# Keeping attention's output in float32, two load queues at the start, and the last output in halves

## Chip, core and metric

The kernel runs on one core of a Trainium2 chip (trn2). The time is the device time of one execution in microseconds (us). TensorE is called PE, VectorE DVE, ScalarE ACT, GpSimd POOL and SyncE SP; on SP only DMA issues appear.

## The reference

Causal attention with B = 2, H = 12, S = 448, D = 64, then two mixture blocks without routing. All arrays are float32.

```python
scores = scale * np.matmul(q, k.transpose(0, 1, 3, 2))
scores = np.where(mask, -1000000000.0, scores)
attn = np.exp(scores - np.max(scores, axis=-1, keepdims=True))
attn = attn / (np.sum(attn, axis=-1, keepdims=True) + 1e-09)
x = np.matmul(attn, v)            # reshaped to 896 tokens x 768
h = x @ w_in                      # 768 -> 2048
x = (h - np.tanh(h)) @ w_out      # 2048 -> 768
a = x @ w_a                       # 768 -> 1536
b = x @ w_b
out = a * b @ w_out2              # 1536 -> 768
```

## The kernel before

**Layout.** Two heads are stacked on 128 partitions, so attention works on 12 pairs (b, p). The output of pair (b, p) is a tile of 128x448 of x: six row blocks kk of 128 features and two batches B0, B1 of 448 tokens. Every float32 product is made of three matmuls over a high and a low part (`matmuls`, L323): high by high, weight-high by x-low, weight-low by x-high. So every operand needs a high part (a cast, on ACT) and a low part (a subtraction, on DVE or POOL). From the second group of the first block on, products run as a 2x2 scheme with seven products, which needs sums and differences of blocks of x.

**Weights.** A part of a weight goes through a pipeline: `load_part` (L175, two SP DMAs into one of three raw buffers), `magnitude` (L188, an ACT cast into `top`), `bits` (L197, a DVE operation that puts the float32 value into a tile `t` and frees the raw buffer), `split_high` (L292, ACT, `wh`) and `split_low` (L301, `wl`, POOL in attention, DVE later). `wh` and `wl` are a ring of five; PE frees an entry when its last matmul with it is done.

**Attention.** Its order is written out by hand in the table ORDER (L23–48), a string of steps. `S` are scores, `L` is mask and minimum on DVE (L431), `X` the exponential on ACT (L440), `T` a transpose on PE (L454) and `C` the copy of its result (ACT L462, DVE L464), `V` the values (L480), `D` the division (L522, L524), which writes x to a tile `x` and its high part to `xh`; `J` makes the low part `xl` (L534). `q`, `k`, `v` are loads on SP (L376, L382). Steps without a pair number are spare steps: `w` two loads of weights, `m` magnitude, `b` bits, `h` and `l` the splits, `f` two matmuls of the first block's hidden layer for batch B0, `g` what follows it. Ahead of the table stand the first loads and WARM = 6 matmuls of zeros (L561, L562).

**After attention** the scheduler orders what is not bound. For kk = 0, 1, 2, `x_sums` (L680) puts x together again as xh + xl for row blocks kk and kk + 3, two adds of 128x896 (L685), and makes four differences of 128x448 from them (L653). `x_terms` (L694) splits these into high and low parts with `halve` (L649, L650). The first group of four hidden blocks runs as plain products for B1, and then, for each of the six blocks dm of w_out, two products of 12 matmuls (four hidden blocks by three), each in a PSUM bank named `s`, `t`, `o` or `h`; ACT copies its bank away (`ypart`, L834) before the bank is used again. Tiles of `g` (`gwh`, `gwl`, 128x896) come from a pool with six of each.

**The end.** The last loop adds up the seven products per row block; for m = 4 `kept` (L883, ACT copy) and `put` (L888, SP DMA) send 128x448 of the output. The very last one is m = 4, n = 2.

Of the kernel before, what the change touches and what calls it, by code (L numbers as in the profile page):

```python
# [9 lines left out]
F32 = mybir.dt.float32  # L10
# [30 lines left out]
L0.9 T20.8 T30.8 S3.10 L2.9 C30.8 X0.9 C20.8 S01.10 b g h V0.8 Q2.11 L3.10 J.6 X1.9 Q3.11 g L1.10 V1.8 v.10 D.8  # L41
T31.9 X2.9 A.9 w H.11 T30.9 C31.9 C30.9 f I.9 l f X3.10 w f T01.9 L0.10 W.9 f f Q1.11 m C01.9 w T21.9 g C21.9
T20.9 C20.9 f f T00.9 m g f f R.9 J.7 X1.10 S2.10 X0.10 S3.11 K.9 C00.9 L2.10 g g L3.11 V1.9 V0.9 X2.10 g S01.11
S2.11 T20.10 f f L0.11 C20.10 g A.10 J.8 L1.11 T31.10 T21.10 X1.11 b C31.10 f I.10 f X0.11 m T30.10 C21.10
T00.10 b C30.10 X3.11 f f W.10 f f D.9 C00.10 L2.11 T01.10 f w X2.11 g A.11 R.10 C01.10 I.11 g m T31.11 K.10
V1.10 W.11 V0.10 T00.11 D.10 f w C31.11 C00.11 f v.11 f T21.11 f T20.11 g f C21.11 g f f T30.11 C20.11 T01.11
C30.11 f J.9 f R.11 C01.11 b V0.11 V1.11 K.11 D.11 g J.11 H.9 g w J.10 g g H.4
# [4 lines left out]
def attention_moe_moe2(ctx, tc, q, k, v, w_in, w_out, w_a, w_b, w_o, out):  # L52
    nc = tc.nc
    B, H, S, D = v.shape
# [5 lines left out]
    WARM = 6  # L60
# [4 lines left out]
    QC = 112  # L65
    NQ = S // QC
    KD = DM // 128
    NPAIR = H // 2
# [20 lines left out]
    s3p = ctx.enter_context(tc.tile_pool(name="s3", bufs=2))  # L89
# [252 lines left out]
    def attention():  # L342
        with ExitStack() as st:
# [147 lines left out]
            def widen(i):  # L491
                r = sums.pop(i)
                sums[i] = sp.tile([QC, NQ, 2, D], F32, tag="wide", name="wide", bufs=2)
                nc.gpsimd.tensor_copy(out=sums[i], in_=r.unsqueeze(3).to_broadcast([QC, NQ, 2, D]))

# [85 lines left out]
    gh, gl, gw, g_full, made = {}, {}, {}, [], set()  # L581
    PIECES = [slice(a, min(a + 512, NT)) for a in range(0, NT, 512)]
    BATCHES = [slice(b * S, (b + 1) * S) for b in range(B)]
    B0, B1 = BATCHES

    def new_g(f):

        if not g_full:
            gh[f, 0], gl[f, 0] = [g_a.tile([128, S], F32R, tag=x, name=x) for x in ("gh", "gl")]
            return  # L590
        g = [g_full[0].tile([128, NT], F32R, tag=x, name=x) for x in ("gwh", "gwl")]
        gw[f] = g
        for b in range(B):
            gh[f, b], gl[f, b] = [t[:, BATCHES[b]] for t in g]

    def hidden(w, cs, hi, lo, h, act, dve):
# [4 lines left out]
        th = ep.tile([128, 512], F32, tag="e", name="e")[:, :n]  # L601
        gg = ep.tile([128, 512], F32, tag="e", name="e")[:, :n]
# [7 lines left out]

    held, fills, rests = [], [], []
# [16 lines left out]
    def load_parts():  # L628
# [5 lines left out]
        "h": split_high, "l": split_low,  # L634
# [7 lines left out]
    g_full.append(ctx.enter_context(tc.tile_pool(name="g2", bufs=max(GROUPS1))))  # L642
# [12 lines left out]
    def etile():  # L655
        return ep.tile([128, 512], F32, tag="e", name="e")[:, :S]
# [23 lines left out]
    def x_sums(kk):  # L680

        sums = []
        for k, tag in ((kk, "gwh"), (kk + NK, "gwl")):
            t = g_full[0].tile([128, NT], F32, tag=tag, name="xsum")
            nc.vector.tensor_tensor(out=t, in0=xh[k].bitcast(F32), in1=xl[k].bitcast(F32), op=ALU.add)  # L685
            sums.append(t)
        (b11, b12), (b21, b22) = [[t[:, cs] for cs in BATCHES] for t in sums]
        minus(b11, b12, b11)
        minus(b12, b22, b12)
        minus(b22, b22, b11)  # L690
        minus(b21, b21, b22)
        return {5: b11, 7: b12, 6: b22, 4: b21}

    def x_terms():  # L694

        for kk in range(NK):
            halve(xh[kk][:, B1], xl[kk][:, B1], sums[kk][5])
            yield
# [59 lines left out]
    def times(u, q, x, on_chip):  # L758
# [10 lines left out]
        if p not in g32:  # L769
            g32[p] = g_full[0].tile([128, NT], F32, tag=("gwh", "gwl")[b], name="g32")  # L770
# [28 lines left out]
    for gi, g in enumerate(GROUPS1):  # L799
        final = gi == len(GROUPS1) - 1  # L800
        if gi == 0:
            sums = {}
            for f in range(g):
                if f < NK:
                    sums[f] = x_sums(f)
                if f % 2 == 0:
                    two = [g_full[0].tile([128, NT], F32R, tag=x, name=x) for x in ("gwh", "gwl")]
# [92 lines left out]
    for m in LAST:  # L900
        for n, u in enumerate(quads):
# [15 lines left out]
            elif m == 7:  # L917
                add(z[n], o)
                put(2 * n + 1, B1, z[n])
            elif m == 4:  # L920
                put(2 * n + 1, B0, kept(o))
# [30 lines left out]
```

## Time and profile before

| what | value |
|---|---|
| median of 3 runs | 547.32 us (546.91 to 547.54) |
| the profiled execution itself | 546.67 us |
| span in its profile | 544.9 us |
| PE busy | 539.3 us, 99% |
| DVE, ACT, POOL busy | 437.9 (80%), 334.3 (61%), 65.4 us (12%) |
| moved by DMA | 64.94 MB, mean 119 GB/s |

The span goes from the first to the last recorded instruction; the time of the execution has a little beside it. Busy time is that of an engine's own instructions; a matmul's end is modelled, so start-to-start distances say more about PE's pace than durations. "Idle before" an instruction is the time in which its engine did nothing, with what ended it.

### The profile page before, as it was taken

To read this page: it belongs to the slowest core of one execution; us is meant where nothing else is said; L and a number is where in the kernel's file an instruction comes from. 1 tells how busy PE (TensorE), PEld (TensorE's weight loads), DVE (VectorE), ACT (ScalarE), POOL (GpSimd) and SP (SyncE) were. 2 spreads that over 40 slices of the span, in tenths; PEclk is the share of its full clock that TensorE was granted. 3 is DMA by queue.
4 is the path that set the end of the run, shared out by engine and by line. 5 is a ranking of instruction groups with operands and counts; after the bars stand their busy time and mean duration, and the time that the engine had idled before them with its cause. 6 is when DMAs were issued, how large, how long until landed. Compare 5 with 4: busy or idle time off the path is not lost.

```text
span 544.9 us, 8643 instructions
## 1 busy us (share of the span) xinstructions
PE 539.3 (99%) x3094; PEld 480.9 (88%) x3094; DVE 437.9 (80%) x855; ACT 334.3 (61%) x688; POOL 65.4 (12%) x88
## 2 busy tenths in 40 slices
PE   8999999999999999999999999999999999999997
PEld 5777788898999899899898899999999999999996
DVE  6888886499889778549879999879798879999840
ACT  6999996466768743238746464756565657356511
POOL 5689761200000000000000000000000000000000
PEclk9999999999999999999999999999999999999999
DMA  8835242145144641313741033637474531001011
GB/s 259 261 102 161 68 133 80 32 161 171 58 130 155 215 137 59 115 59 96 225 143 59 0 116 117 209 111 241 136 251 135 190 116 58 2 0 52 17 69 67
DMA packets 70827, 64.94 MB, mean 119 GB/s; under 512 B 13952, under 2 KB 70784, under 8 KB 70784
## 3 DMA queue, kind: packets, MB, share of 16 engines
q1 hardware_dynamic: 70784, 64.40, 37.3%
q8 instruction: 24, 0.39, 0.3%
q14 instruction: 19, 0.16, 0.1%
HBM read 61.63 MB, written 2.75 MB: 118 GB/s over the span
## 4 chain that ended last, share of the span: by engine, by line
PE 98%; ACT 1%; DVE 0%; issue 0%; DVEq 0%
PE s L328 43%; PE t L328 19%; PE h L328 14%; PE o L328 8%; PE o L480 5%; PE s L419 4%; PE t L454 4%; PE t L499 1%; PE h L454 1%; PE h L562 1%; ACT p L440 0%; DVE p L431 0%; ACT ypart L834 0%; ACT e L885 0%; DVE warm L355 0%
## 5 line engine op out<-in xcount | busy, mean ns | idle before, releaser
L292 ACT CAST wh<-t 128x384 fp32r<-128x384 f32 (+2 forms) x141 | 77.1, 577 | 49.3 <-PE s L328 24.4
L194 ACT CAST top<-raw 128x768 f16<-128x768 bf16 (+1 forms) x70 | 73.9, 1056 | 48.5 <-DMA raw<-in_moe_w_b 12.9
L301 DVE TENSOR_TENSOR wl<-t,wh 128x384 fp32r<-128x384 f32 (+2 forms) x136 | 82.1, 625 | 15.5 <-ACT wh L292 15.2
L214 DVE SCALAR_TENSOR_TENSOR t<-raw,top 128x768 int32<-128x768 int32 (+1 forms) x62 | 58.6, 960 | 0.4 <-ACT top L194 0.2
L440 ACT ACTIVATE p<-p,m 112x448 f32<-112x448 f32 (+3 forms) x96 | 50.0, 528 | 4.5 <-DVE m L431 4.2
L328 PE MATMUL s<-last,wh 128*128 128x448 f32 x168 | 48.4, 365 | 0.0
L328 PE MATMUL s<-xl,wh 128*128 128x448 f32 x120 | 44.0, 366 | 0.0
L328 PE MATMUL s<-xh,wl 128*128 128x448 f32 x120 | 43.5, 365 | 0.0
L328 PE MATMUL s<-xh,wh 128*128 128x448 f32 x120 | 43.4, 366 | 0.0
L431 DVE CUSTOM_DVE_ANT_0 p<-s,mask 112x448 f32<-112x448 f32 (+3 forms) x96 | 37.9, 440 | 6.3 <-PE s L419 5.7
L328 PE MATMUL s<-gwh,wl 128*128 128x384 f32 (+2 forms) x96 | 34.9, 365 | 0.0
L328 PE MATMUL s<-gwl,wh 128*128 128x384 f32 (+2 forms) x96 | 34.8, 364 | 0.0
L328 PE MATMUL s<-gwh,wh 128*128 128x512 f32 (+2 forms) x96 | 34.3, 364 | 0.0
L328 PEld LDWEIGHTS s<-last,wh 128*128 128x128 f32 x168 | 31.5, 188 | 2.6
L328 PE MATMUL s<-last,wl 128*128 128x448 f32 x84 | 30.7, 365 | 0.0
L745 DVE TENSOR_TENSOR e<-s,e 128x448 f32<-128x448 f32 x31 | 19.2, 619 | 12.7 <-PE s L328 12.4
L454 PE MATMUL t<-ident,p 112*112 112x112 f32 x195 | 27.6, 265 | 0.2 <-ACT p L440 0.2
L480 PE MATMUL o<-pt,v 112*64 112x224 f32 (+1 forms) x288 | 26.1, 326 | 0.0
L462 ACT COPY pt<-t 112x448 f32<-112x448 f32 (+1 forms) x39 | 18.5, 485 | 11.8 <-PE t L454 10.2
L649 ACT CAST last<-g 128x896 fp32r<-128x896 f32 x21 | 19.0, 942 | 10.4 <-PE t L328 4.5
L401 POOL TENSOR_TENSOR qkl<-qk,qkh 128x448 fp32r<-128x448 f32 x22 | 25.2, 1147 | 1.0
L454 PEld LDWEIGHTS t<-ident,p 112*112 112x112 f32 x195 | 19.9, 133 | 5.7 <-issue 1.1
(219 smaller groups left out, 1459.8 us busy)
## 6 DMA issues: line engine op xcount, KB each, us to landing
raw<-in_moe_w_out SPq DMA_DIRECT2D x48, 383.2 KB, 4.1
raw<-in_moe_w_in SPq DMA_DIRECT2D x32, 383.2 KB, 4.0
raw<-in_moe_w_a SPq DMA_DIRECT2D x24, 383.2 KB, 4.1
raw<-in_moe_w_b SPq DMA_DIRECT2D x24, 383.2 KB, 4.9
raw<-in_moe_w_out SPq DMA_DIRECT2D x12, 255.5 KB, 3.2
qk<-in_q SPq DMA_DIRECT2D x12, 224.0 KB, 3.8
qk<-in_k SPq DMA_DIRECT2D x12, 224.0 KB, 4.5
v<-in_v SPq DMA_DIRECT2D x24, 112.0 KB, 3.3
```

The source lines that it names most:

```text
L194: nc.scalar.copy(out=tops[i % len(tops)][:, 0:nk, :, 1], in_=top[:, :, :, 2])
L214: nc.vector.scalar_tensor_tensor(out=ts[i], in0=low[:, :, :, 0], scalar=13, in1=top, op0=ALU.logical_shift_right, op1=ALU.bitwise_or)
L292: nc.scalar.copy(out=halves[j][0], in_=x)
L301: engine.tensor_tensor(out=lo, in0=source(j), in1=hi.bitcast(F32), op=ALU.subtract)
L328: nc.tensor.matmul(o, a, b_, start=j == 0 and not go_on, stop=j == n - 1, skip_group_check=True)
L401: nc.gpsimd.tensor_tensor(out=lo[:, x], in0=qk[i][:, x], in1=hi[:, x].bitcast(F32), op=ALU.subtract)
L419: nc.tensor.matmul(sc[i, c][e], a[r, 0, cs], b_[r, 1, :n], start=x == 0, stop=x == len(terms) - 1)
L431: nc.vector.tensor_tensor_reduce(out=p[:, e], in0=s, in1=mask[:QC, S - n:], scale=-scale, scalar=3.0e38, op0=ALU.add, op1=ALU.min, accum_o ...
L440: nc.scalar.activation(out=p[:, e], in_=p[:, e], func=ACTF.Exp, bias=least[i][:, c, e:e + 1], scale=-1.0, accum_out=sums[i][:, c, e:e + 1],)
L454: nc.tensor.transpose(out=pst[:QC, x * QC:(x + 1) * QC], in_=blk, identity=ident[:QC, :QC])
L480: nc.tensor.matmul(o[64 * e:64 * e + 64, cs], vt[:, k_, e, :], p.rearrange("s c q -> s (c q)"), start=k_ == 0, stop=k_ == 2 * h + 1, skip_ ...
L745: nc.vector.tensor_tensor(out=x, in0=o, in1=x, op=ALU.add)
```

## The change

1. **x in float32.** `divide` writes x into tiles of the g ring, in float32, and they stay there. `x_sums` with its adds is gone. Its twelve differences are made in place by a generator `early_sums`, a step of which stands in ORDER as `P` (six times); the rest follow through `x_terms`.
2. **Room and order.** The g ring is split: a pool with three of each is there from the start, one with three more opens after attention, together with the `s3` pool. Tiles `e` are 448 instead of 512 wide, `wide` has one buffer instead of two, `x` is gone. In ORDER, `w`, `m` and `b` stand earlier in the last seven lines, and there is one more of each.
3. **Loads.** The host lays v out with rows of 512 numbers for a pair; from the third pair on its v is one DMA, before that two. The k of pairs 0 and 1 is issued by ACT. WARM is 5.
4. **The end.** The last output is copied and sent in two halves of 224 columns, the first by SP, the second by ACT's queue.

```diff
 ORDER = """
...
-S2.11 T20.10 f f L0.11 C20.10 g A.10 J.8 L1.11 T31.10 T21.10 X1.11 b C31.10 f I.10 f X0.11 m T30.10 C21.10
...
+g S01.11 S2.11 T20.10 m f f L0.11 C20.10 g A.10 J.8 L1.11 P T31.10 T21.10 X1.11 b C31.10 w m P f I.10 f X0.11
...
-    WARM = 6
+    WARM = 5
...
             def fetch(i, nm):
                 b, p = pairs[i]
                 if nm == "v":
-                    for e in range(2):
-                        nc.sync.dma_start(
-                            out=vs[i % NV][:, :, e, :], in_=v[b, 2 * p + e].rearrange("(c s) d -> s c d", s=QC)
-                        )
+                    for x in (slice(0, 1), slice(1, 2)) if i < 2 else (slice(0, 2),):
+                        nc.sync.dma_start(out=vs[i % NV][:, :, x], in_=v[b, p][:, :, x])
                     return
                 if nm == "q":
                     qk[i] = inp.tile([128, 2, S], F32, tag="qk", name="qk")
-                nc.sync.dma_start(
+                queue = nc.scalar if i < 2 and nm == "k" else nc.sync
+                queue.dma_start(
...
             def divide(i):
-                xs[i] = sp.tile([128, S], F32, tag="x", name="x", bufs=2)
+                b, k = pairs[i]
+                if k not in x32:
+                    x32[k] = g_tile("gwh" if k < EARLY else "gwl", F32)
+                xs[i] = x32[k][:, BATCHES[b]]
...
+    EARLY = KD // 2
+    g_early = ctx.enter_context(tc.tile_pool(name="g1", bufs=EARLY))
...
+    def g_tile(tag, dt=F32R):
+
+        n = g_count.get(tag, 0)
+        g_count[tag] = n + 1
+        pool = g_early if n % max(GROUPS1) < EARLY else g_full[0]
+        return pool.tile([128, NT], dt, tag=tag, name=tag)
...
+    def early_sums():
+
+        def minus_x(kk, x):
+            (b11, b12), (b21, b22) = [[x32[k][:, cs] for cs in BATCHES] for k in (kk, kk + EARLY)]
+            o, p, q = ((b11, b12, b11), (b12, b22, b12), (b22, b22, b11), (b21, b21, b22))[x]
+            nc.vector.tensor_tensor(out=o, in0=p, in1=q, op=ALU.subtract)
+            sums[kk] = {5: b11, 7: b12, 6: b22, 4: b21}
+
+        for kk in range(EARLY):
+            minus_x(kk, 0)
+            yield
+        for kk in range(EARLY):
+            for x in (1, 2, 3):
+                minus_x(kk, x)
+                yield
...
-    g_full.append(ctx.enter_context(tc.tile_pool(name="g2", bufs=max(GROUPS1))))
+    s3p = ctx.enter_context(tc.tile_pool(name="s3", bufs=2))
+    g_full.append(ctx.enter_context(tc.tile_pool(name="g2", bufs=max(GROUPS1) - EARLY)))
...
-    def x_sums(kk):
-
-        sums = []
-        for k, tag in ((kk, "gwh"), (kk + NK, "gwl")):
-            t = g_full[0].tile([128, NT], F32, tag=tag, name="xsum")
-            nc.vector.tensor_tensor(out=t, in0=xh[k].bitcast(F32), in1=xl[k].bitcast(F32), op=ALU.add)
...
             elif m == 4:
-                put(2 * n + 1, B0, kept(o))
+                rows = slice((2 * n + 1) * 128, (2 * n + 2) * 128)
+                for queue, cs in ((nc.sync, slice(0, S // 2)), (nc.scalar, slice(S // 2, S))):
+                    e = etile()[:, 0:S // 2]
+                    nc.scalar.copy(out=e, in_=o[:, cs])
+                    queue.dma_start(out=out[rows, cs], in_=e)
```

Three places of the order of instructions, before and after. In the rows a name is a tile, its number the instance.

SP at the very start, before:

```order
L382 DMA qk<-in_q 128x448
L382 DMA qk<-in_k 128x448
L382 DMA qk<-in_q 128x448
L382 DMA qk<-in_k 128x448
L376 DMA v_99<-in_v 112x4x64 x2
L382 DMA qk<-in_q 128x448
L382 DMA qk<-in_k 128x448
```

and after:

```order
L378 DMA qk<-in_q 128x448 x2
L373 DMA v_99<-in_v 112x4x64 x2
L378 DMA qk<-in_q 128x448
L378 DMA qk<-in_k 128x448
L373 DMA v_100<-in_v 112x4x64 x2
L182 DMA raw<-in_moe_w_in 128x3x511 x2
```

The loads of k for pairs 0 and 1 have left SP's queue; the q of pair 1 stands second, and v follows at once. ACT's queue after the change begins with them, ahead of the load of its table:

```order
L378 DMA qk<-in_k 128x448 x2
L436 ACT_TABLE_LOAD
L436 ACTIVATE p,sum<-p,m 112x448 [waits DVE_49] x2
L436 ACTIVATE p,sum<-p,m 112x336 [waits DVE_49] x2
L458 COPY pt_103<-t 112x4x112 [waits PE_49]
```

DVE just after attention, before. `wl` are the low parts of weight blocks of w_out, each the work of one split:

```order
L301 TENSOR_TENSOR wl<-t,wh 128x512
L650 TENSOR_TENSOR tl<-xsum,th 128x448
L653 TENSOR_TENSOR xsum<-xsum 128x448
L301 TENSOR_TENSOR wl<-t,wh 128x512
L214 SCALAR_TENSOR_TENSOR t<-raw,top_84 128x512
L301 TENSOR_TENSOR wl<-t,wh 128x512
L650 TENSOR_TENSOR tl<-xsum,th 128x448
L650 TENSOR_TENSOR xl<-xsum,xh 128x448
L214 SCALAR_TENSOR_TENSOR t<-raw,top_83 128x768
L650 TENSOR_TENSOR gl<-xsum,gh 128x448
L214 SCALAR_TENSOR_TENSOR t<-raw,top_84 128x768
L301 TENSOR_TENSOR wl<-t,wh 128x512
```

and after:

```order
L624 TENSOR_TENSOR gwl<-gwl 128x448 x2
L298 TENSOR_TENSOR wl<-t,wh 128x512 x3
L676 TENSOR_TENSOR gl<-gwl,gh 128x448
L211 SCALAR_TENSOR_TENSOR t<-raw,top_81 128x512
L676 TENSOR_TENSOR xl<-gwh,xh 128x448
L211 SCALAR_TENSOR_TENSOR t<-raw,top_80 128x768
L676 TENSOR_TENSOR xl<-gwh,xh 128x448 x2
L298 TENSOR_TENSOR wl<-t,wh 128x512
L612 TENSOR_TENSOR e<-h,e 128x448
L211 SCALAR_TENSOR_TENSOR t<-raw,top_81 128x768
```

The adds of 128x896 are gone, the first three `wl` stand in a row instead of being spread over other steps, and the fourth comes behind the `xl`.

PE at the third dm block, before. `gh` and `gl` are the hidden layer's parts, `o` and `t` banks:

```order
L328 MATMUL t_2005<-gl_1687,wh_1824 128x448
L328 MATMUL t_2005<-gh_1686,wl_1825 128x448
L328 MATMUL o_2134<-gh_1146,wh_1947 128x448 [waits Activation_49]
L328 MATMUL o_2134<-gl_1147,wh_1947 128x448
L328 MATMUL t_2092<-gh_1146,wh_1912 128x448 [waits Activation_49]
L328 MATMUL t_2092<-gl_1147,wh_1912 128x448
L328 MATMUL t_2092<-gh_1146,wl_1913 128x448 [waits DVE_49]
L328 MATMUL t_2092<-gh_1419,wh_1912 128x448
L328 MATMUL t_2092<-gl_1420,wh_1912 128x448
```

and after:

```order
L325 MATMUL t_1980<-gl_1680,wh_1814 128x448
L325 MATMUL t_1980<-gh_1679,wl_1815 128x448
L325 MATMUL o_2108<-gh_1137,wh_1921 128x448 [waits Activation_49]
L325 MATMUL o_2108<-gl_1138,wh_1921 128x448
L325 MATMUL o_2108<-gh_1137,wl_1922 128x448 [waits DVE_49]
L325 MATMUL o_2108<-gh_1407,wh_1921 128x448
```

Before, the block in `o_2134` is broken off after two matmuls and the block in `t_2092` goes in between; the matmul that the split `wl_1948` holds up comes after it. Now the block in `o_2108` follows the block in `t_1980` and runs through; eight more of its matmuls follow, and then the block in `t_2066`, whose first matmul waits for ACT.

## Rows read from the trace of the kernel before

**Rows 1.** The page, part 4: the chain that ended last, by engine.

```profile
PE 98%; ACT 1%; DVE 0%; issue 0%; DVEq 0%
```

**Rows 2.** PE's waits: line, what for, total us, times, longest us.

```profile
PE h L562 <- DVE warm L355: 1.3, 1, 1.3
```

**Rows 3.** Windows: us, busy of each engine (instructions), PEclk, DMA share, GB/s.

```profile
0.00:4.00 4.00, 2.74 (x7) 0.77 (x7) 2.10 (x4) 1.28 (x1) 0.97 (x7) 1.00 0.52 142
4.00:8.00 4.00, 3.47 (x21) 1.93 (x21) 2.72 (x13) 2.06 (x7) 2.33 (x4) 1.00 1.00 285
75.00:109.00 34.00, 34.00 (x269) 29.20 (x264) 20.02 (x57) 21.66 (x63) 9.39 (x12) 1.00 0.21 61
109.00:150.00 41.00, 40.78 (x201) 37.46 (x201) 39.33 (x66) 27.32 (x52) 0.00 (x0) 1.00 0.39 129
150.00:540.00 390.00, 390.00 (x1925) 357.90 (x1924) 317.24 (x512) 218.34 (x368) 0.00 (x0) 1.00 0.35 114
```

**Rows 4.** Timeline of the start: start us, us, engine, line, operation.

```profile
0.79 1.28 ACT L440 ACT_TABLE_LOAD   x1 [0.79 <-PEq L935]
0.80 0.39 SPq L382 DMA_DIRECT2D qk<-in_q  x1
1.24 0.42 SPq L382 DMA_DIRECT2D qk<-in_k  x1
1.25 2.74 PE L562 MATMUL h<-warm 128*128 128x512 bf16 x6 [1.25 <-DVE warm L355]
4.00 1.71 PE L419 MATMUL s<-qk 64*112 64x448 f32 x8
```

**Rows 5.** Line L382 in 0.7:1.2 us (q of pair 0), then in 1.21:1.68 (its k).

```profile
DMA to landing us min/median/max: 2.5/2.5/2.5
...
DMA to landing us min/median/max: 2.6/2.6/2.6
```

**Rows 6.** DVE's groups by form, the adds and subtractions of x: count, busy us, mean ns.

```profile
L653 DVE TENSOR_TENSOR xsum<-xsum 128x448 f32<-128x448 f32 x12 | 7.2, 617 | 0.0
L685 DVE TENSOR_TENSOR xsum<-xh,xl 128x896 f32<-128x896 f32 x6 | 6.3, 1082 | 0.0
```

**Rows 7.** Timeline of DVE around the end of attention.

```profile
91.10 0.51 DVE L464 COPY pt<-t 112x336 f32<-112x336 f32 x1 [2.89 <-PE t L454]
105.63 0.51 DVE L464 COPY pt<-t 112x336 f32<-112x336 f32 x1 [3.62 <-PE t L454]
109.00 0.62 DVE L522 TENSOR_TENSOR x<-o,y 128x448 f32<-128x448 f32 x1 [1.66 <-PE o L480]
109.54 0.61 DVE L524 TENSOR_TENSOR xh<-o,y 128x448 fp32r<-128x448 f32 x1
```

**Rows 8.** Timeline of ACT, PE and DVE at the third dm block.

```profile
112.90 1.08 ACT L194 CAST top<-raw 128x768 f16<-128x768 bf16 x1 [4.42 <-DMA raw<-in_moe_w_in]
...
122.33 0.69 DVE L301 TENSOR_TENSOR wl<-t,wh 128x512 fp32r<-128x512 f32 x1
122.46 0.53 ACT L834 COPY ypart<-t 128x448 f32<-128x448 f32 x1 [0.62 <-PE t L328]
122.46 0.36 PE L328 MATMUL o<-gl,wh 128*128 128x448 f32 x1
123.05 0.47 PE L328 MATMUL t<-gh,wh 128*128 128x448 f32 x1 [0.22 <-ACT ypart L834]
123.36 0.36 PE L328 MATMUL t<-gl,wh 128*128 128x448 f32 x1
```

**Rows 9.** Timeline of the end; landing of its transfer (L889); ACT's copy of 336 columns.

```profile
541.62 0.53 ACT L885 COPY e<-s 128x448 f32<-128x448 f32 x1 [3.12 <-PE s L328]
542.17 0.33 SPq L889 DMA_DIRECT2D out<-e  x1
...
DMA to landing us min/median/max: 1.9/1.9/1.9
...
L462 ACT COPY pt<-t 112x336 f32<-112x336 f32 x18 | 7.9, 438 | 4.6 <-PE t L454 4.4
```

More of the change, by code (lines that the diff above doesn't have):

```diff
@@ L492, in widen @@
                 r = sums.pop(i)
-                sums[i] = sp.tile([QC, NQ, 2, D], F32, tag="wide", name="wide", bufs=2)
+                sums[i] = sp.tile([QC, NQ, 2, D], F32, tag="wide", name="wide", bufs=1)
                 nc.gpsimd.tensor_copy(out=sums[i], in_=r.unsqueeze(3).to_broadcast([QC, NQ, 2, D]))
@@ L590, in new_g @@
             return
-        g = [g_full[0].tile([128, NT], F32R, tag=x, name=x) for x in ("gwh", "gwl")]
+        g = [g_tile(x) for x in ("gwh", "gwl")]
         gw[f] = g
@@ L609, in now @@
         f()
+    def early_sums():
[11 more added lines that the diff above has]
+                yield
+    early = early_sums()
     held, fills, rests = [], [], []
@@ L633, in attention_moe_moe2 @@
         "f": fill, "g": lambda: rests.pop(0)(), "w": load_parts, "m": magnitude, "b": bits,
-        "h": split_high, "l": split_low,
+        "h": split_high, "l": split_low, "P": lambda: next(early),
     }
@@ L655, in etile @@
     def etile():
-        return ep.tile([128, 512], F32, tag="e", name="e")[:, :S]
+        return ep.tile([128, S], F32, tag="e", name="e")[:, :S]
     def small(n=1):
@@ L678, in rights_of @@
                 r[m] = [x[k][:, cs] for x in (hi, lo)]
-    def x_sums(kk):
-        sums = []
-        for k, tag in ((kk, "gwh"), (kk + NK, "gwl")):
-            t = g_full[0].tile([128, NT], F32, tag=tag, name="xsum")
-            nc.vector.tensor_tensor(out=t, in0=xh[k].bitcast(F32), in1=xl[k].bitcast(F32), op=ALU.add)
[L686 to L692, printed above, removed]
     def x_terms():
         for kk in range(NK):
+            for _ in early:
+                pass
             halve(xh[kk][:, B1], xl[kk][:, B1], sums[kk][5])
@@ L769, in times @@
         if p not in g32:
-            g32[p] = g_full[0].tile([128, NT], F32, tag=("gwh", "gwl")[b], name="g32")
+            g32[p] = g_tile(("gwh", "gwl")[b], F32)
         nc.vector.tensor_tensor(out=g32[p][:, BATCHES[f % 2]], in0=x, in1=left.pop(q), op=ALU.mult)
@@ L801, in attention_moe_moe2 @@
         if gi == 0:
-            sums = {}
             for f in range(g):
-                if f < NK:
-                    sums[f] = x_sums(f)
                 if f % 2 == 0:
-                    two = [g_full[0].tile([128, NT], F32R, tag=x, name=x) for x in ("gwh", "gwl")]
+                    two = [g_tile(x) for x in ("gwh", "gwl")]
                 gh[f, 1], gl[f, 1] = [t[:, BATCHES[f % 2]] for t in two]
@@ L919, in attention_moe_moe2 @@
                 put(2 * n + 1, B1, z[n])
+            elif m == 4 and n < NK - 1:
+                put(2 * n + 1, B0, kept(o))
             elif m == 4:
-                put(2 * n + 1, B0, kept(o))
+                rows = slice((2 * n + 1) * 128, (2 * n + 2) * 128)
[3 more added lines that the diff above has]
+                    queue.dma_start(out=out[rows, cs], in_=e)
             for _ in range(AHEAD[n]):
@@ L936 @@
     arrays, args = {}, []
+    b, h, s, d = inputs["v"].shape
+    v = inputs["v"].reshape(b, h // 2, 2, s // 112, 112, d).transpose(0, 1, 4, 3, 2, 5)
     for name in _INS:
-        a = np.ascontiguousarray(inputs[name] if name == "v" else inputs[name].transpose(0, 1, 3, 2))
+        a = np.ascontiguousarray(v if name == "v" else inputs[name].transpose(0, 1, 3, 2))
         arrays["in_" + name] = a
```

26 lines of the change are left out of this document (11 added, 15 removed).

## Prediction

> **What bounds the kernel now.** I read the chain of waits first. Followed back from the last instruction, 98% of the span lies on PE (TensorE) [rows 1], so nothing gains that does not shorten PE's own line. The list of PE's waits comes next: its longest, 1.3 us, is for DVE's memset of the warm tile, which the change leaves alone [rows 2]. The windows then say where PE stands still. From 150 to 540 us it is busy for 390.00 of 390.00 us with 1925 matmuls, 0.203 us each; in 75–109 us it has no idle time either. What is left is in 0–4 us (2.74 busy, warm-up alone), 4–8 us (3.47 of 4.00), and 109–150 us (40.78 of 41.00) [rows 3]. After 540 us comes the tail, one copy and one transfer. So a change that keeps PE's matmuls as they are, as this one does but for one warm matmul of zeros, can win or lose only in these places, and each is worth about 1 us at most.
>
> DVE (VectorE) is second: 39.33 of 41 us in 109–150, but 20.02 of 34 in 75–109 [rows 3]. That matters because the change moves DVE work from the full stretch into the empty one.
>
> **The start.** SP issues the q of pair 0 at 0.80 us and its k at 1.24; PE's first score matmul runs at 4.00, after six warm matmuls in 1.25–3.99 [rows 4]. q took 2.5 us to land and k 2.6 [rows 5]: q is there at 3.30, k at 3.84, and PE begins 0.16 later. ScalarE now issues k while SP issues q. Lower bound of the cost: if k landed with q, PE could begin at 3.46, but five warm matmuls end only at about 3.99 − 2.74/6 = 3.53, so the gain is at most about 0.45 us. Upper bound: both transfers share the DMA engines and both come late, by at most about the half of k's issue gap, +0.2. The rows do not show two queues in parallel. The DMA engines are busy for 0.52 × 4 = 2.1 us of 0–4 us [rows 3], 3.2 us of which lie behind the first issue: up to 1.1 us may have been free for k's bytes, unless no byte can come so soon. Between the ends nothing decides, so I take the middle of "nothing" and −0.45: **−0.25 us**. ScalarE pays two DMA issues (0.42 each on SP, the same operation) ahead of its table load of 1.28 us, which ends at 2.07 now and at 2.9 then [rows 4]; an exponential cannot start before the scores, at 4.00 now and 3.55 at the earliest then, so the load stays covered by 0.6 us or more, and if that cover went, each exponential would start later by what is missing. Pair 1's k goes the same way, and its q moves up on SP by 0.44. The start gains in full only if the work behind it also moves up, with no transfer that holds it back; I count it in full.
>
> **The v loads.** 24 SP issues become 14; the ten pairs after the first two come in rows of 2 KB instead of 256 B. This frees SP and DMA time. PE's list of waits names no transfer, so its price is 0; the v of the last pair would show it first, as it now stands behind two raw loads on SP, whose buffers DVE frees earlier.
>
> **x in float32: six adds gone, twelve subtractions moved.** DVE loses 6 adds of 128x896, 6.3 us, and keeps 12 subtractions, 7.2 us [rows 6]; eight of them now run inside attention. Two stand before a transpose copy that DVE waits for until 91.10 (idle 2.89 us), with two weight steps beside them; four stand before the copy at 105.63 (idle 3.62 us) [rows 7]. 2 × 0.6 + 0.7 and 4 × 0.6 fit with 1.0 us to spare in each, so they cost 0; uncovered, a subtraction is 0.6 us late for the mask step behind it. The 6.3 us are no gain by themselves, since PE was not waiting for DVE; they are a gain only through the next item.
>
> **The stall at 123.05 us.** In the third dm block PE ran two matmuls into bank o, the second at 122.46, changed to bank t and had to wait until ScalarE had copied t away (0.53 us from 122.46); the t matmul ran at 123.05 instead of 122.66 [rows 8]. It costs 0.39, and the restart behind it 0.11, as the next matmul came 0.31 instead of 0.20 later [rows 8]: 0.50 in all. PE changed banks there because the weight part wl of block o was split by DVE only at 122.33–123.02 [rows 8]. In the new order the o block runs all 12 matmuls in one go, and the t block comes 10 matmuls (2.0 us) later, so that the copy of t is long done. The new cover is o's wl. From 109.00 DVE issues 0.54 apart [rows 7]: thirteen steps to 116.0, three wl (0.69 each less the 0.08 by which neighbours overlap) to 117.8, then six steps (four of 0.54, two weight steps estimated by their columns at 0.6 and 0.9) to 121.5, o's wl done at 122.1; PE wants it at 122.66. ScalarE must also have o's bank copied by 122.26: its chain there (wh at about 119.4, since PE frees the ring then; tanh; a cast of 1.08 [rows 8]; the copy of 0.53) ends at about 121.8. Margins of 0.5 us, so I take the full **−0.50**; bounds −0.5 and, if the raw load comes as late as now, +0.9 (rival 3).
>
> **The other stalls after 109 us.** 41.00 − 40.78 is 0.22 [rows 3], all in that wait; 0.00 in 150–540. The scheduler's new order of blocks there moves no PE work: 0, bounds ±0.4, which is four restarts of 0.1.
>
> **The tail.** The last matmul is followed by one ScalarE copy at 541.62 (0.53 us) and one SP transfer at 542.17, which lands 1.9 us later [rows 9]. A ScalarE copy takes 0.53 us for 448 columns and 0.438 for 336 [rows 9], 0.8 ns a column, so 0.35 for 224: the second half is ready at 542.32, 0.15 later than the whole now, but its transfer is half as large. At the 285 GB/s of 4–8 us [rows 3] its 229 KB take 0.80 of the 1.9 us, so half of them save up to 0.40. Net between −0.25 and +0.15, I take **−0.10**.
>
> **Sum.** −0.25 − 0.50 − 0.10 = −0.85 us. The profiled execution took 546.67, 0.65 below the median of 547.32; it would become 545.82, and against the median the forecast is **546.5 us**. The 0.2% that a measurement of this kernel can tell is 1.09 us, so the forecast is a gain just under what can be told: 546.23 is the bound.
>
> **Rivals.** 1. *The forecast*, 546.2 to 546.8 by its bounds: chance 0.48, a third of it below 546.23.
>
> 2. *The start gives nothing.* k's bytes follow q's on engines that are already full: two loads of 229 KB at 285 GB/s need 1.6 us, and 0.52 × 4 = 2.1 us is all the full work there was [rows 3]. Issuing k sooner then only interleaves the two, and PE waits for the later one at 3.84 as before. Time: 547.32 − 0.60 = 546.7. Chance 0.17. The Trainium skill, page "DMA: Bandwidth & Descriptors", section "Issuing engines are not separate DMA queues", says that transfers started by different engines run on the same 16 DMA engines and interleave, so that only the time to issue is saved. By that rule the start is worth 0 and the time is this rival's; no run here yet shows two queues, and the share of 0.52 leaves both open.
>
> 3. *The stall only moves.* If the 768-wide raw load reaches ScalarE at 112.90 as now [rows 8], the casts behind it come about a microsecond later, o's wl is ready at about 124.1 and twelve matmuls queue behind it: +1.4 for −0.5. Against it: its buffer is freed by a DVE step that now runs near 94 us instead of 106. Time 547.32 − 0.35 + 0.9 = 547.9. Chance 0.05, within 0.2%.
>
> 4. *More than forecast.* The whole 0.45 at the start, 0.5 in the middle, 0.25 in the tail and 0.4 of restarts: −1.6, 545.7. For it: every term has its bound there. Chance 0.20.
>
> 5. *Slower: PE stays at its lower clock.* The warm matmuls of 512 columns come 2.74/6 = 0.46 us apart, the 1.2 GHz level, and the main stretch runs 448 columns in 0.203 us, the 2.4 GHz level [rows 3, 4], although the granted clock reads 1.00 in both. Now there is one warm matmul fewer, and if k lands late PE stands idle between 3.53 and 4.00 where it ran without a gap. If the rise came later for that, matmuls of 4–8 us would take double: 3.47 us more, less the 0.53 of waits there [rows 3], at most +2.9. It decides from +1.7, where the 0.6 of the other terms are eaten and 1.09 lost. Middle of 1.7 and 2.9: 547.32 − 0.6 + 2.3 = 549.0. For it: the rise itself lies near this point. Against it: a gap of 0.4 us is short, and it is gone if k lands early. Chance 0.10.
>
> **How the numbers follow.** Faster: 0.20 and a third of 0.48, 0.36. Slower: 0.10. Same: 0.54. The range runs from 545.4, rival 4 with the measurement's spread of 0.3 to 0.4, to 547.9, rival 3; only rival 5 and some of the ends lie outside.
>
> **What would show it.** Right: first score matmul near 3.75; t's first matmul of the fourth block follows without a wait, and PE's list has no ypart row; 109–150 with no idle time for PE; the last copy ending at 542.3. Wrong: a score matmul at 4.0 or later; score matmuls after it at half pace; o's wl behind 122.7; a PE wait for exponentials or mask steps in 84–106 us, which would mean that the moved subtractions and weight steps were not covered.

## The result and the profile after

The changed kernel took a median of **549.86 us** (549.24 to 551.29 in five executions); the kernel before, on the same chip, 547.33 (546.91 to 547.62 in five). The ratio, taken over all executions and not from the two medians, is 1.0053 with an interval of 1.0043 to 1.0064, so it is slower, and above the forecast's range. The profiled execution took 549.24 us with a span of 547.5; that is the fastest of its five, 0.62 below their median.

The page of the changed kernel, busy times and the chain by engine:

```profile
PE 541.4 (99%) x3093; PEld 481.8 (88%) x3093; DVE 432.8 (79%) x849; ACT 334.6 (61%) x689; POOL 65.9 (12%) x88
...
PE 94%; ACT 3%; DVE 2%; DMA 1%; issue 1%; POOL 0%; POOLq 0%; ACTq 0%; DVEq 0%
```

DVE lost 5.1 us (437.9 before), most of the 6.3 of its six adds [rows 6], and PE, which sets the end, gained 2.1 (539.3 before). The chain lay on PE for 98% [rows 1] and now does for 94%: ACT, DVE and a DMA stand in it, among them k's load and the first exponentials (3.66 and 2.53 us of the chain). PE's list of waits names that DMA; columns as in [rows 2]:

```profile
PE h L561 <- DVE warm L352: 1.2, 1, 1.2
PE s L415 <- DMA qk<-in_k: 0.9, 1, 0.9
PE t L495 <- ACT pt L458: 0.2, 1, 0.2
```

The wait for `ypart` is gone and one of 0.9 us for pair 0's k has come. The windows, with the columns of [rows 3]:

```profile
0.00:4.00 4.00, 2.32 (x5) 0.59 (x5) 2.10 (x4) 1.28 (x1) 0.97 (x7) 1.00 0.50 140
4.00:8.00 4.00, 3.50 (x12) 1.80 (x14) 1.51 (x5) 0.84 (x3) 2.50 (x4) 1.00 1.13 342
...
109.00:150.00 41.00, 41.00 (x214) 36.96 (x211) 32.76 (x58) 29.33 (x55) 0.00 (x0) 1.00 0.46 146
150.00:540.00 390.00, 390.00 (x1923) 357.63 (x1922) 313.78 (x506) 216.38 (x365) 0.00 (x0) 1.00 0.34 110
```

Three things are to be seen. In 109–150 us PE has no idle time any more (40.78 before). In 4–8 us it is busy as long as before, 3.50 against 3.47, but the records show 12 matmuls instead of 21: they run at a lower pace. The column PEclk reads 1.00 there, but it counts time without a clock record as full. The trace's records of full clock, the 2.4 GHz level, begin only at 8.52 us; before, they begin at 4.31. So nearly all of pair 0's scores now run at the lower level. And in the first 4 us the DMA engines moved no more than before, 140 GB/s against 142.

The timeline of the changed kernel's start:

```profile
0.79 0.90 ACTq L378 DMA_DIRECT2D qk<-in_k  x2
0.80 0.87 SPq L378 DMA_DIRECT2D qk<-in_q  x2
1.25 2.32 PE L561 MATMUL h<-warm 128*128 128x512 bf16 x5 [1.25 <-DVE warm L352]
...
4.50 4.42 PE L415 MATMUL s<-qk 64*112 64x448 f32 x16 [0.93 <-DMA qk<-in_k]
7.16 0.67 ACT L436 ACTIVATE p<-p,m 112x448 f32<-112x448 f32 x1 [4.14 <-DVE m L427]
8.85 0.88 PE L450 MATMUL t<-ident,p 112*112 112x112 f32 x7
...
DMA to landing us min/median/max: 3.5/3.6/3.7
```

The last line is the landing of pair 0's two loads; q is the 3.5, k the 3.7. Rows of the same operations in the kernel before:

```profile
4.00 1.71 PE L419 MATMUL s<-qk 64*112 64x448 f32 x8
5.97 1.37 PE L419 MATMUL s<-qk 64*112 64x112 f32 x8 [0.26 <-DVE m L431]
...
5.95 0.67 ACT L440 ACTIVATE p<-p,m 112x448 f32<-112x448 f32 x1 [3.87 <-DVE m L431]
7.50 0.97 PE L454 MATMUL t<-ident,p 112*112 112x112 f32 x7 [0.17 <-ACT p L440]
...
75.24 0.61 DVE L604 TENSOR_TENSOR e<-h,e 128x448 f32<-128x448 f32 x1
...
76.26 0.45 PE L328 MATMUL h<-xh,wh 128*128 128x448 f32 x1
```

k is issued 0.45 us sooner and lands 0.6 later: its load takes 3.7 instead of 2.6 us [rows 5], and q's 3.5 instead of 2.5. PE waits 0.93 us after the last warm matmul and begins at 4.50. From there the 16 score matmuls of pair 0 take 4.42 us, where they took 3.34 (4.00 to 7.34). So the first exponential is 1.21 us later (7.16 against 5.95), the first transpose 1.35 (8.85 against 7.50).

Following the same matmul in both traces tells where the rest came from. The lag, by how much it starts later in the changed kernel, is:

| matmul (time before, time after, us) | lag | what was added |
|---|---|---|
| first score (4.00, 4.50) | 0.50 | k's landing |
| first transpose (7.50, 8.85) | 1.35 | the lower clock; 1.21 at the transposes behind it |
| first `h` matmul behind J.6 (76.26, 78.05) | 1.79 | 0.30 in one step there, the rest a tenth at a time |
| second matmul after attention (109.09, 111.00) | 1.91 | 0.1 |
| last matmul (541.21, 543.73) | 2.52 | −0.5 for the stall, about +1.4 from a slower pace, −0.3 of small restarts |

### The profile page after: what moved, and what is told of

Read it like the earlier page. It is cut to its first block, busy times and chain, and to the rows that moved or that the text cites. A ratio compares the mean times of both kernels' runs of the same rounds, so it can differ in the third digit from the quotient of the medians.

```text
span 547.5 us, 8626 instructions
## 1 busy us (share of the span) xinstructions
PE 541.4 (99%) x3093; PEld 481.8 (88%) x3093; DVE 432.8 (79%) x849; ACT 334.6 (61%) x689; POOL 65.9 (12%) x88
## 4 chain that ended last, share of the span: by engine, by line
PE 94%; ACT 3%; DVE 2%; DMA 1%; issue 1%; POOL 0%; POOLq 0%; ACTq 0%; DVEq 0%
PE s L325 42%; PE t L325 18%; PE h L325 14%; PE o L325 8%; PE o L476 3%; PE s L415 3%; PE t L450 3%; ACT p L436 2%; PE t L495 1%; DMA qk<-in_k 1%; DVE p L427 1%; PE h L450 0%; ACT pt L458 0%; DVE t L211 0%; ACT top L191 0%
## 5 line engine op out<-in xcount | busy, mean ns | idle before, releaser
L476 PEld LDWEIGHTS o<-pt,v 112*64 112x64 f32 x288 | 18.7, 136 | 7.1 <-issue 0.9
```

The lines of the kernel that those rows point to most:

```text
L476: nc.tensor.matmul(o[64 * e:64 * e + 64, cs], vt[:, k_, e, :], p.rearrange("s c q -> s (c q)"), start=k_ == 0, stop=k_ == 2 * h + 1, skip_ ...
```

## The experiments

Two theories stood against each other for the start. One: sharing the DMA engines makes k late, and the idle PE pays again, as the full clock and with it the pace of the score matmuls comes late. The other: the start only shifts by what k is late, and the time is lost elsewhere, in the subtractions moved into attention or in the main stretch. Times are medians of 11 or 12 executions on one of three chips, each with the kernel before on the same chip (547.17, 547.70 or 547.26 there), and there is one profile of each kernel.

### The start, taken apart

The changed kernel with the start of the kernel before:

```diff
-    WARM = 5
+    WARM = 6
...
-                queue = nc.scalar if i < 2 and nm == "k" else nc.sync
-                queue.dma_start(
+                nc.sync.dma_start(
```

> The changed kernel with its start as before: both k loads on SP and six warm matmuls; all else stays changed. Theory A (the start costs: the k of pair 0 lands 0.6 us later with two queues, PE stands idle from 3.57 to 4.50 and its full clock comes at 8.52 instead of 4.31 us, so the first exponential runs 1.2 us later): first score matmul at 4.0, full clock near 4.3, first exponential near 5.95, and the time falls by 1.2 to 1.8 us from 549.86, to 548.0 to 548.7. Rival B (the loss is in the new order and in PE's slower pace after 110 us, 207 instead of 203 ns a matmul): the start moves but the time falls by less than 0.6, to above 549.2. Rival C (the start is all of it): 547.3 or less.

Measured: 547.13 us against 547.17, ratio 1.0003 (0.9994 to 1.0012). The first score matmul runs at 4.08, full clock is recorded from 4.48, the first exponential runs at 6.07. Without the new start nothing is left that can be measured, which is what rival C said. The fall from 549.86 holds more than the start, though: the slower pace of which more below is in the first profile and not in this one. What is left of the other terms cancels: below.

Then the changed kernel with more warm matmuls, k still on ACT (`WARM = 6`, `WARM = 7`):

> The changed kernel with six warm matmuls, the k loads still on ScalarE's queue. The warm matmuls end at 3.99, the first score stays at 4.50 because k lands late, so PE is idle for 0.5 instead of 0.9 us. Theory A1 (the warm matmul decides when the full clock comes): full clock at 4.3 to 5 us, the first scores at full pace, first exponential near 6.5 instead of 7.16, time 549.1 to 549.4. Theory A2 (any gap ahead of the scores does it): full clock still near 8.5, time 549.7 to 550.

> The changed kernel with seven warm matmuls, the k loads still on ScalarE's queue: the warm matmuls end at about 4.4 and no gap is left before the first score at 4.50. Theory A: the full clock comes near 4.3, the first exponential near 6.45; what is left of the start's loss is the 0.5 us by which k is late, time near 549.1. If the clock has no part in it and only the late k counts: first exponential at 7.1, time near 549.9.

Measured: 547.84 and 547.83 against 547.17, ratios 1.0010 (1.0001 to 1.0018) and 1.0010 (1.0001 to 1.0019). The sixth warm matmul wins back 0.66 of the 1.21 us at the first exponential, the seventh nothing more; full clock is recorded from 5.06 and 4.89. In the medians it cannot be told how much that is, since the changed kernel itself had 1.0053 once and 1.0017 (1.0004 to 1.0030) once, below. Timeline of the kernel with six:

```profile
4.33 1.91 PE L415 MATMUL s<-qk 64*112 64x448 f32 x8 [0.34 <-DMA qk<-in_k]
6.52 1.37 PE L415 MATMUL s<-qk 64*112 64x112 f32 x8 [0.28 <-DVE m L427]
...
6.50 0.67 ACT L436 ACTIVATE p<-p,m 112x448 f32<-112x448 f32 x1 [3.49 <-DVE m L427]
```

The 16 score matmuls now take 3.56 us (4.33 to 7.89) instead of 4.42, but k is still late, and PE begins 0.33 after the kernel before.

Next the kernel before with the new start alone:

```diff
-    WARM = 6
+    WARM = 5
...
-                nc.sync.dma_start(
+                queue = nc.scalar if i < 2 and nm == "k" else nc.sync
+                queue.dma_start(
```

> The kernel before with the changed start alone: k of pairs 0 and 1 on ScalarE's queue and five warm matmuls. Theory A: the first score at 4.5, full clock near 8.5, first exponential near 7.15, time 1.2 to 1.6 above before, 548.5 to 548.9. Rival B (the start is made good later, the loss is in the order): within 0.5 of 547.3.

Measured: 547.98 against 547.17, ratio 1.0018 (1.0009 to 1.0027): by itself, the start costs 0.8 us. Its trace, PE at the start and at the third dm block:

```profile
4.27 4.36 PE L420 MATMUL s<-qk 64*112 64x448 f32 x16 [0.71 <-DMA qk<-in_k]
...
124.52 0.47 PE L328 MATMUL t<-gh,wh 128*128 128x448 f32 x1 [0.22 <-ACT ypart L835]
```

The slow score matmuls are here too (4.36 us for 16, full clock from 8.17), and the stall of [rows 8] is still there, 1.47 us later, since this kernel has the old order.

The opposite cut leaves one warm matmul out and gives k back to SP (`queue` as in the first experiment, `WARM = 5`):

> The changed kernel with both k loads back on SP and five warm matmuls: k lands near 3.9 again, the first score at 4.0, PE idle for 0.43 us ahead of it (e2 had six warm matmuls and a gap of 0.34, with full clock at 5.06; e4 five and 0.70, with full clock at 8.17). Theory G1 (the missing sixth warm matmul decides): full clock near 8, first exponential near 6.7, time 547.8 to 548.2. Theory G2 (the length of the gap decides, and below half a us it is harmless): full clock near 4.8, first exponential near 6.1, time near 547.2.

Measured: 548.57 against 547.70, ratio 1.0014 (1.0001 to 1.0026). It was to part the warm matmul's share from the queue's, and it could not: in its profiled execution k landed at 4.47 although SP had issued it alone, so PE waited 1.0 us here as well, full clock came at 9.14 and the first exponential ran at 7.24. It is one more case of a gap behind five warm matmuls with slow scores after it, and no more.

### Why two queues bring pair 0 later

Either pair 1's loads, which now run beside pair 0's from the start, take its bandwidth; or two queues don't bring k sooner whatever stands behind them. Two kernels, both with `WARM = 6` and only pair 0's k on ACT. The first also holds pair 1's loads back until POOL has written its tile, and it alone has the two lines of the `memset`:

```diff
+                if i == 1 and nm == "q":
+                    nc.gpsimd.memset(qk[i][:, 0], 0.0)
-                queue = nc.scalar if i < 2 and nm == "k" else nc.sync
+                queue = nc.scalar if i < 1 and nm == "k" else nc.sync
```

> The changed kernel with six warm matmuls, k of pair 0 on ScalarE's queue, and the loads of pair 1 held back on SP behind a POOL memset of their tile, so that for about a us only q and k of pair 0 are under way. Theory H1 (k lands late because pair 1's loads share the DMA engines with it; the first bytes come no sooner): q and k both land near 3.9 to 4.0, first score near 4.05, first exponential near 6.0, time near 547.3. Theory H2 (two queues are slow to begin by themselves): k still at 4.3 or later. Theory H3 (with nothing beside it the second queue gains, as was forecast): k at 3.6 or before, first score at 4.0, held there by the sixth warm matmul.

> The changed kernel with six warm matmuls and only the k of pair 0 on ScalarE's queue; pair 1's q and k follow on SP at once. Theory H1: q of pair 1 now runs beside k of pair 0, but its k no longer does; k of pair 0 lands at 4.1 to 4.3, between e9 and e2, first score at 4.15 to 4.35, time 547.3 to 547.8. Theory H2: k at 4.3 or later, as in e2.

Measured: 547.84 and 547.76 against 547.26, ratios 1.0009 (1.0000 to 1.0018) and 1.0007 (0.9998 to 1.0015). Landing of pair 0's q and k, and its score matmuls, with pair 1 held:

```profile
DMA to landing us min/median/max: 3.2/3.3/3.4
...
4.25 2.23 PE L417 MATMUL s<-qk 64*112 64x448 f32 x8 [0.27 <-DMA qk<-in_k]
```

and with pair 0's k alone on ACT:

```profile
DMA to landing us min/median/max: 3.4/3.5/3.6
...
4.41 4.05 PE L415 MATMUL s<-qk 64*112 64x448 f32 x16 [0.42 <-DMA qk<-in_k]
```

With pair 1 held until 2.46 us, k still lands 3.4 us after its issue, at 4.21, between what the two theories gave; with pair 0's k alone on ACT it lands at 4.37, as H2 said. The five other profiles with two queues have 4.23 to 4.45. So holding pair 1 back moves k by no more than these differ among themselves, and pair 1 is not shown to be the cause. With one queue k, issued 0.45 later, landed at 3.86 to 4.03 in five profiles, and at 4.47 in the one of the experiment above. What goes with the later landing is the pairing.

The windows of the first transfers show where it arises, in the kernel before and then in the changed one (columns as in [rows 3]):

```profile
0.00:1.75 1.75, 0.50 (x2) 0.23 (x3) 0.70 (x2) 0.96 (x1) 0.70 (x7) 1.00 0.00 0
1.75:2.50 0.75, 0.75 (x3) 0.21 (x2) 0.70 (x1) 0.33 (x1) 0.27 (x1) 1.00 0.70 158
2.50:3.75 1.25, 1.25 (x4) 0.30 (x2) 0.70 (x1) 0.00 (x0) 0.00 (x0) 1.00 1.05 323
...
1.75:2.50 0.75, 0.75 (x3) 0.21 (x2) 0.70 (x1) 0.75 (x1) 0.27 (x1) 1.00 0.83 55
2.50:3.75 1.25, 1.06 (x3) 0.15 (x1) 0.70 (x1) 0.51 (x1) 0.00 (x0) 1.00 0.89 334
```

No byte moves before 1.75 us. In the next 0.75 the engines are busy in both, 0.70 and 0.83, but with two queues they move 55 GB/s instead of 158; from 2.50 on the rates are alike. Over all profiles that stretch has 55 to 112 GB/s with two queues and 112 to 258 with one. It is not all of the delay: at 112 in both, k landed at 3.93 from one queue (the moved `P`, below) and at 4.29 from two (six warm matmuls).

The Trainium skill, page "DMA: Bandwidth & Descriptors", section "Issuing engines are not separate DMA queues", has transfers of different engines interleave on the same 16 DMA engines, with only issue time saved. These landings agree that the two loads interleave (they end 0.2 us apart), except that here the saving, 0.45 us of k's issue, was more than lost. Why the first bytes come more slowly from two queues stays open, and so does the one late landing with one queue.

### The first subtraction

In the first experiment's profile the largest step of lag inside attention, 0.30 us, stands where the first `P` is. DVE and PE's weight loads there (that kernel; L623 is the subtraction, L611 the sum `e<-h,e`, which frees bank `h`):

```profile
75.13 0.61 DVE L532 TENSOR_TENSOR xl<-gwh,xh 128x448 fp32r<-128x448 f32 x1
75.67 0.61 DVE L623 TENSOR_TENSOR gwh<-gwh 128x448 f32<-128x448 f32 x1
76.20 0.61 DVE L611 TENSOR_TENSOR e<-h,e 128x448 f32<-128x448 f32 x1
...
76.87 0.19 PEld L325 LDWEIGHTS h<-xh,wh 128*128 128x128 f32 x1 [0.28 <-DVE e L611]
```

Before, `e<-h,e` ran at 75.24, straight behind `xl`, and PE had no wait at 76.26. Now the subtraction stands between them and PE waits 0.28. In ORDER, `P` follows `J.6` by one step and the `g` that brings the sum comes after it. So this `P` was moved on, on top of the old start:

```diff
-... J.6 X1.9 P Q3.11 g L1.10 V1.8 v.10
+... J.6 X1.9 Q3.11 g L1.10 V1.8 v.10
...
-... J.8 L1.11 P T31.10 T21.10 X1.11 ...
+... J.8 L1.11 P P T31.10 T21.10 X1.11 ...
```

> e1 (start as before) with the first P of the order moved from behind J.6 to the place of the second P. In e1 PE waits 0.28 us near 76.9 for DVE's e<-h,e, which frees bank h and which stands behind this first subtraction. Theory F (the moved subtraction cost that wait): no PE wait near 76.9, PE 0.3 us earlier from there on, time 0.3 below e1, near 546.85. Rival (the wait is another's, a mask step or the exponentials): PE's times at 95 us stay those of e1, time as e1, 547.1.

Measured: 547.43 against 547.70, ratio 0.9993 (0.9983 to 1.0003). The step of 0.30 is gone from the trace, but the medians don't show it against the kernel before. Another wait stood in its profile; ACT's cast of a raw part and PE's transposes:

```profile
13.97 1.07 ACT L191 CAST top<-raw 128x768 f16<-128x768 bf16 x1 [0.97 <-DMA raw<-in_moe_w_in]
...
17.33 0.50 PE L449 MATMUL t<-ident,p 112*112 112x112 f32 x3 [0.63 <-ACT pt L457]
```

ACT stood 0.97 us for a raw load, and the copy behind it came late for PE. SP had issued that load's two parts at 6.45 to 7.6, before the change at 5.68 to 7.1 (SP's timeline in both), since two issues of v in the new layout take 1.24 to 1.35 us on SP where they took 0.97. The same kernel with v in the old layout, two loads a pair:

```diff
-                    for x in (slice(0, 1), slice(1, 2)) if i < 2 else (slice(0, 2),):
-                        nc.sync.dma_start(out=vs[i % NV][:, :, x], in_=v[b, p][:, :, x])
+                    for e in range(2):
+                        nc.sync.dma_start(
+                            out=vs[i % NV][:, :, e, :], in_=v[b, 2 * p + e].rearrange("(c s) d -> s c d", s=QC)
+                        )
```

> e6 (start as before, first P later) with the v loads and their layout as before. In e6 and e8 SP issued the first weight part at 6.45 instead of 5.68 us, because the two v loads of a pair took longer to issue, and it landed at 13.7 to 13.9 instead of 12.55; in e6 ScalarE waited 0.97 us for it. Theory I (the v loads cost that margin): the second weight transfer issued near 6.7, landed before 12.9, no ScalarE wait for it, and PE runs ahead of the kernel before by 0.3 to 0.5 us after 130 us: time 0.3 to 0.5 below the kernel before, and below e6's distance to it. Rival (the landing varies by itself): issue times as in e6, or the wait stays.

Measured: 547.46 against 547.26, ratio 1.0005 (0.9996 to 1.0014). The parts are issued from 5.70, the cast runs at 12.87 with no wait, as at 12.86 before. The late cast was not in every profile of the new layout (not in the first experiment's), so the layout takes a margin and now and then a wait; the medians don't show the gain of 0.3 to 0.5 that was expected. This profile has the slower pace of the last experiment in it.

### The end

The kernel of the moved `P` with the old single copy and transfer at the end (`put(2 * n + 1, B0, kept(o))`):

> e6 with the end as before, too: one copy and one transfer for the last output. In the profiles from the last matmul's start to the last landing it takes 2.88 us with one transfer and 2.84 to 2.92 with two halves. Theory: the halves are worth nothing, time as e6 within 0.15 us, near 546.8. Rival: the halves do gain 0.1 to 0.3 and the time rises by that against e6.

Measured: 547.85 against 547.70, ratio 1.0002 (0.9992 to 1.0012); its sibling with halves had 547.43. The difference of 0.4 is not in the tail: from the start of the last matmul to the last landing it takes 2.95 us here and 2.88 in its sibling, and 2.88 in the kernel before and 2.86 in the changed one. This execution began slowly, with the old start (full clock from 7.13, first exponential at 6.79), and ended at a slower pace from about 495 us on, of which more below. The changed kernel's tail, and the landing of its two halves:

```profile
544.13 0.59 ACT L937 COPY e<-s 128x224 f32<-128x224 f32 x2 [3.12 <-PE s L325]
544.50 0.33 SPq L938 DMA_DIRECT2D out<-e  x1
544.76 0.35 ACTq L938 DMA_DIRECT2D out<-e  x1
...
DMA to landing us min/median/max: 1.7/1.8/1.8
```

A transfer of half the size lands 1.7 to 1.8 us after its issue, the whole took 1.9 [rows 9]. The second half is issued 0.63 us after the first copy starts, the whole was issued 0.55 after its own, so the one uses up nearly all that the other saves.

### The same kernel again, and a slower pace

> The changed kernel itself, unaltered, with more executions. Its first profile held two losses that the kernels e1 to e4 split: the late start (about +1.2 us at the first exponential) and, from 111 to 182 us, 206.7 instead of 202.7 ns from matmul to matmul (about 345 matmuls by 4 ns, +1.4 us), which none of e1 to e4 showed. Theory D (the slower pace comes by chance, set anew in each execution at the restart near 111 us): times in two groups, near 548 and near 549.5, and a profile with either pace. Theory E (the slower pace belongs to this kernel's timing): all times near 549.3 or above, and the pace is there again.

Measured, with nothing changed: 548.11 against 547.70, ratio 1.0017 (1.0004 to 1.0030). Eight of twelve executions took 547.83 to 548.31, four 549.16 to 550.86. So the first five, 549.24 to 551.29, all lie where only four of these twelve do, and no experiment tells why. A profile of each kind is at hand, 549.24 and 548.09. But for the end of pair 0's scores, where they part by up to 0.33 us (full clock from 8.52 and from 7.84), they agree within 0.05 us from 12 to 111 us. Windows of the first (columns as in [rows 3]):

```profile
135.00:155.00 20.00, 20.00 (x98) 18.18 (x97) 16.20 (x30) 14.80 (x29) 0.00 (x0) 1.00 0.37 119
155.00:175.00 20.00, 20.00 (x98) 18.17 (x97) 12.86 (x24) 11.60 (x23) 0.00 (x0) 1.00 0.25 79
```

and of the second:

```profile
135.00:155.00 20.00, 20.00 (x101) 18.54 (x100) 16.45 (x30) 15.31 (x30) 0.00 (x0) 1.00 0.36 119
155.00:175.00 20.00, 20.00 (x100) 18.53 (x99) 13.59 (x25) 11.70 (x24) 0.00 (x0) 1.00 0.25 79
```

PE is busy without a gap in both, but these 40 us show 196 matmuls in the first and 201 in the second (one that runs across an edge counts on both sides). Their starts in the timeline, two of the same product ten matmuls apart, say it per matmul; the first execution, then the second:

```profile
111.20 0.37 PE L325 MATMUL t<-xh,wl 128*128 128x448 f32 x1
...
113.26 0.37 PE L325 MATMUL t<-xh,wh 128*128 128x448 f32 x1
```

```profile
111.16 0.36 PE L325 MATMUL t<-xh,wl 128*128 128x448 f32 x1
...
113.19 0.36 PE L325 MATMUL t<-xh,wh 128*128 128x448 f32 x1
```

That is 206 ns against 203 each, and over longer stretches of the starts 206.7 against 202.7. It lasts from the restart behind the values' matmuls at 111 us to about 181 us, some 340 matmuls by 4 ns, 1.4 us. The last matmul of the second execution stands at 542.60, 1.13 sooner than the first's 543.73, as some restarts there cost the second 0.27. From 185 to 265 us both show 396 matmuls. The granted clock is recorded as full through all of it in both. As program and place are the same and only the execution differs, the pace does not come from the program alone; whether the change makes it more frequent is not shown. The kernel of the moved `P` with the old v loads shows it between 109 and 179 us, the one with five warm matmuls and k on SP and the one with the old tail from about 495 us to the end, worth 0.9 us each. These two take it up without a break in PE's stream.

## Why the prediction was wrong

**The start: the step that failed.** It was priced at −0.25 us, "the middle of nothing and −0.45", with +0.2 as the upper end. It measured +1.2 at the first exponential and +1.35 at the first transpose in the changed kernel (+1.2 at both in the repeated profile), and alone in the kernel before +1.0 at the first exponential and 0.8 in the median. Two of the prediction's own signs came: the first score matmul behind 4.0, and score matmuls at half pace. Two sizes were off. The landing of k got 0.6 later, not "the half of k's issue gap" at the most: the DMA share of 0.52 was read as room for k's bytes, but no byte moves before 1.75 us, and behind that the share was 0.70 and then 1.05, so there was little room; and in 1.75–2.50 us the changed kernel moved a third of what the one before did. And the pace of the scores, which was kept apart as a rival, belongs to the same step, since a late k makes the gap that goes with it, and one warm matmul fewer makes it longer: full clock from 8.52 us instead of 4.31.

**Rival 5 named the mechanism**, with a chance of 0.10 and the first of its two arguments against it, that a gap of 0.4 us is short, resting on a gap that came out as 0.93. It read the granted clock as 1.00 at the warm matmuls, where the trace has no record. Its price was too high: 0.85 between first score and first transpose (1.35 − 0.50), not 2.3, since from the first transposes on the upper pace was back (seven of them in 0.88 us, 0.97 before). Its result, 549.0, lies between the measured 549.86 and 548.11, but by luck and other terms: the slower pace in the main stretch, which no rival held, gave 1.4 in the first, and a late k and the first subtraction, which it did not hold either, gave 0.5 and 0.3.

**Rival 2 had the rule right and the time wrong.** The two loads interleave and two queues save nothing in landing. But saved issue time is not 0 by itself, it is the 0.45 us of k's issue here, and the landing, which it took as unchanged at 3.84, was 4.2 to 4.5.

**The subtractions at 0: wrong for one of twelve.** The prediction weighed the six between 84 and 106 us, and those did hide: DVE still waits for PE at the two copies, with less idle time than in [rows 7], 2.89 and 3.62 before:

```profile
93.01 0.51 DVE L460 COPY pt<-t 112x336 f32<-112x336 f32 x1 [1.92 <-PE t L450]
...
107.53 0.51 DVE L460 COPY pt<-t 112x336 f32<-112x336 f32 x1 [1.26 <-PE t L450]
```

The first one, at 76 us, stands ahead of the sum that frees bank `h`. The prediction does not weigh it, and it cost 0.30: one step of 0.6 less the slack there.

**The v loads at 0: right in price, wrong in cover.** PE's list named no transfer, but a raw load behind them had about 0.3 us to spare (landed at 12.55, cast at 12.86), and in the profile of the moved `P` it came late, for 0.6 us of PE's time. In the one with pair 1 held it did so too, but there the holding itself delayed its issue, to 7.12.

**The middle stall at −0.50: right.** The 109–150 window went from 40.78 to 41.00, the list of waits has no `ypart` row, and in the repeated profile the lag falls by 0.48 across the place (1.87 to 1.39). Its new cover held as reckoned; ACT, DVE and PE there:

```profile
123.21 0.53 ACT L845 COPY ypart<-o 128x448 f32<-128x448 f32 x1
...
123.24 0.68 DVE L298 TENSOR_TENSOR wl<-t,wh 128x512 fp32r<-128x512 f32 x1
...
124.42 0.37 PE L325 MATMUL o<-gh,wh 128*128 128x448 f32 x1
...
124.84 0.37 PE L325 MATMUL o<-gh,wl 128*128 128x448 f32 x1
```

The copy ends at 123.74 for a matmul at 124.42, `wl` at 123.92 for one at 124.84: margins of 0.7 and 0.9 where 0.5 was expected. Rival 3 fell with it.

**The tail at −0.10: 0 measured**, inside its bounds. Half of the bytes saved 0.1 to 0.2 of the landing, not "up to 0.40".

Together: with the repeated profile, +1.2 at the first transpose, +0.30 at the first subtraction, −0.5 at the stall and +0.4 in small steps give +1.4 (542.60 − 541.21). The medians of those executions say +0.4 (548.11 − 547.70) and the ratio over all of them +0.9; the kernel before had its own executions at two levels there, near 547.4 and 548.2. With the first profile, 1.1 more for the slower pace. So of the 2.5 us between the first profile and the one before (543.73 − 541.21) the start explains about half.

**What stays open.** What sets the pace of the main stretch in an execution, and why all of the first five had times of the upper kind; and when exactly the full clock comes. It is recorded from 7.84 to 9.14 us in the four profiles with five warm matmuls, whose gaps are 0.7 to 1.0. With six, it is 4.16 behind a gap of 0.16, 7.13 behind one of 0.17, 5.06 behind 0.34 and 6.75 behind 0.42. So the gap alone doesn't settle it, and since the one kernel that was to part k's queue from the missing warm matmul had a late k too, their shares are not shown. And no kernel here beat the one before by what can be told: the best, the old start with the moved `P`, had 0.9993 (0.9983 to 1.0003).

## What to carry to other kernels

Before a load is put on a second queue, ask whether the bytes or the issue set its landing, with the DMA share read from the first byte on and not from the program's start, and take the pair's landing as the later of the two or worse until a trace shows two queues. Warm-up matmuls should reach to the moment at which the first real operand lands, so a change that can delay that load should not shorten them. A step that hides in DVE's idle time is hidden only if nothing behind it in the queue frees a bank that PE wants next: go through every place where it is put, not the longest idle times.

## What the hardware showed that was not expected

- Loads of pair 0 from two queues landed later than from one: q 3.5 us after issue instead of 2.5, k 3.7 instead of 2.6, with pair 1 held back 3.2 and 3.4. In their first 0.75 us the engines moved 55 GB/s instead of 158.
- The same matmuls of 448 columns run for tens of microseconds at 202.7 or at 206.7 ns each, in two executions of one kernel, with the granted clock at 1.00 in both. The slower pace began behind a short break of PE's stream in two profiles and without one in two others, and costs about 1 us in 50.
- 16 score matmuls take between 3.19 and 4.65 us at the start, as full clock is recorded from 4.16 us on or only from 9.14; the column PEclk shows 1.00 all the while. Warm matmuls of 512 columns come 0.43 us apart (their weight loads at 2.08, 2.51 and 2.93 us), the 1.2 GHz level; the 0.46 of the prediction is their busy time divided by six. 448 columns in 0.203 us are at the 2.4 GHz level.
- An output transfer of half the size landed 1.7 to 1.9 us after its issue, the whole 1.9 to 2.0.
